# Attention into a two-expert mixture: x kept in token order, 16-byte routing records, later gathers, loads on two engines, a gate over four tiles

## The chip, the cores and the metric

The kernel runs on one core of one Trainium2 chip. The metric is the device time of that core in microseconds (us), the median of three runs. The engines are named as in the profile: PE is TensorE, DVE is VectorE, ACT is ScalarE, POOL is GpSimd and SP is SyncE; SPq and ACTq are the queues on which SP and ACT issue transfers.

## The reference

Two stages follow each other. The first is attention within chunks of 64 positions, for 8 batches and 8 heads of width 64. The second is a mixture of 8 experts over the 4608 tokens that the first one gives, in which each token goes to the two experts with the highest noisy logits.

```python
scores = q_c @ k_c.T / sqrt(64)                 # per batch, head and chunk of 64
attn = exp(scores - max); attn /= attn.sum() + 1e-9
x = (attn @ v_c)  as (4608, 512)                # one row a token, heads side by side
noisy = x @ w_gate + log1p(exp(x @ w_noise)) * noise          # (4608, 8)
top2 = the two largest; top2_w = softmax over these two
for e in range(8):
    out[mask] += top2_w * (relu(x[mask] @ w1[e]) @ w2[e])     # 512 -> 1024 -> 512
```

## The kernel before

**Attention.** The tokens are 36 tiles of 128. `attend(it)`, here called a turn, works on several tiles at once: scores of tile `it` (L355), probabilities times v of `it - 2` (`pv`, L381), the transposes of p of `it - 1` (`p_trans`, L371), the transposes of x of `it - 3` (`x_trans`, L396) and the gate logits of `it - 4` (`gate_mm`, L409), all of them on PE in this order. ACT copies the transposed p out of PSUM (`pts`, L373), takes the exponential (`pr`, L367) and copies the transposed x (`xt`, L400). VectorE takes the row maxima, subtracts them (L364), and normalises the product into a tile of x (`xs`). Each tile needs one load of q (`qb`, L320), two of k (`kb`, L322, a lower and an upper half of 64 rows) and two of v (`vb`, L327). SP issues all five, into rings of six buffers, three or four turns ahead.

**Routing.** The tiles form six groups of 4, 8, 4, 4, 8 and 8. When the logits of a group stand, a generator `route(g)` is started. `step_route` takes one VectorE instruction of it at a time at fixed places between other work. It ranks the tokens and gives each of a token's two choices a slot in the list of its expert. A GpSimd indirect transfer then scatters a tile's rows into DRAM (`slots`, L532), two transfers per token tile, 72 in all. A row is 2060 bytes: 512 values of x, a code (token number and second expert) and the two weights. Scatters have places of their own between other work (`scatter`), and a tiny copy or memset on GpSimd ahead of each (L528, L530) holds it back until the named buffer is written.

**Experts.** Each of 8 experts has three blocks of three or four tiles of 128 slots; the list of the blocks over all experts is numbered from 0. `layer1` forms relu(x W1) in eight column blocks of 128, `layer2` the product with W2, tile by tile. Values and weights are split into a high and a low part, and each product is three matmuls (`three`, L263). In layer 1, ACT writes the high part of the hidden values (`hh`, L276) and VectorE the residual (`hl`, L277); three PSUM banks are in turn. `weigh` (L283) multiplies a finished tile by its token weights and `store` adds it to the output through a GpSimd indirect transfer (L230). `w_load` (L107, L109) loads weights from SP and `w_split` splits them.

Blocks 0 and 1 belong to the first expert, and by `EARLY = {0: 2, 1: 4}` their slots are full as soon as the scatters of groups 2 and 4 have landed, block 2's with the last group's. Right behind these scatters SP loads the block's tiles (`xg`, L202) and the three columns of codes and weights (`meta0`). `resolve_early` turns these columns into row numbers and weights on VectorE, just ahead of the block's layer 2, where the store needs them. From block 3 on, SP loads each tile by an offset that is known only then (the expert's place), in four pieces of 32 rows (L207). VectorE transposes such a tile (L250), while PE transposes those of blocks 0 to 2 (L246). `resolve_all` gives the row numbers of all later blocks ahead of block 2's layer 2. Up to LEAD = 7 tiles are loaded ahead (`gather_more`).

**Order of the work.** The order is written out by hand: what the program names first is first on its engine. Turns 0 to 36 come first, then two `x_tile` (transpose and split of a tile of block 0), turn 37, the other `x_tile` and layer 1 of block 0. Inside that layer, `hook_tail` places the last two turns between the first matmuls, and `hook1` two scatters behind each column block. Layer 2 of blocks 0 and 1 has `hook2_r`: a scatter at every second step and the next block's `x_tile` at the places of `TURNS`. SP also writes 37 blocks of zeros into the output (`zero_out`) in that stretch.

## Time and profile before

| | value |
|---|---|
| time, median of 3 runs | 1029.89 us (1028.78 to 1033.22) |
| the profiled execution's own time | 1029.36 us |
| its span in the profile | 1027.6 us |
| PE, matmuls | 983.1 us busy, 96% |
| VectorE (DVE) | 446.1 us, 43% |
| ScalarE (ACT) | 271.3 us, 26% |
| GpSimd (POOL) | 227.4 us, 22% |
| mean granted clock of TensorE | 0.991 |
| DMA | mean 129 GB/s; HBM read 81.69 MB, written 50.13 MB |

A busy PE need not be PE at its peak, and a share of the whole span averages over two stages: attention with routing at the start, and the experts, which take most of the span. A row of the timeline has its start, its length (both in us), the engine, the line, the operation with output and inputs by their names, the tile's shape, and the count; in square brackets stands the idle time ahead of it and what ended it. A row of the table by stretches has the stretch and its length, then the busy time and the number of instructions of PE, of PE's weight loads, of VectorE, ACT and GpSimd, and then the granted clock, the DMA engines' mean share and the GB/s.

### The profile page before, as it was taken

The page shows a single profiled execution, that of the slowest core. Times are in us where ns is not written, and L with a number is a line of the kernel's source. Part 1 is how long each engine was busy: PE and PEld are TensorE (multiplying, and loading weights), DVE is VectorE, ACT ScalarE, POOL GpSimd, SP SyncE. Part 2 cuts the span into 40 slices and gives each one's busy share as a digit, 9 for nine tenths or more (in the row PEclk, how much of TensorE's full clock was granted, in tenths as well). Part 3 has the DMA queues.
Part 4 walks back from the last instruction along what each step waited for, and adds up shares of the span by engine and source line. Part 5 has one row for each costly group of instructions (what it writes and reads, how often), then busy time and mean ns, then how long its engine had stood idle before and what let it go on. Part 6 is the DMA issues. An engine that isn't in the chain of part 4 may idle for free.

```text
span 1027.6 us, 16132 instructions
## 1 busy us (share of the span) xinstructions
PE 983.1 (96%) x5962; PEld 883.5 (86%) x5962; DVE 446.1 (43%) x1005; ACT 271.3 (26%) x542; POOL 227.4 (22%) x332
## 2 busy tenths in 40 slices
PE   6889998999799999999999999999999999999996
PEld 6778887898689889888988998899889998999884
DVE  6656665522525443344334432453245324533311
ACT  3434443211314121222222321232123212322100
POOL 3034754751020111111111102101211111101112
PEclk9999999999899999999999999999999999999998
DMA  8899999864561552264225422553244324412213
GB/s 226 259 292 298 328 323 396 310 177 121 88 166 56 124 117 37 60 140 116 40 46 138 124 40 44 125 135 59 36 121 123 74 43 126 120 21 32 31 21 43
DMA packets 103218, 132.93 MB, mean 129 GB/s; under 512 B 22848, under 2 KB 56000, under 8 KB 103136
## 3 DMA queue, kind: packets, MB, share of 16 engines
q1 hardware_dynamic: 86704, 93.54, 30.4%
q0 software_dynamic: 16432, 38.33, 19.1%
q8 instruction: 48, 0.79, 0.3%
q14 instruction: 34, 0.28, 0.1%
HBM read 81.69 MB, written 50.13 MB: 128 GB/s over the span
## 4 chain that ended last, share of the span: by engine, by line
PE 84%; SPq 6%; DMA 5%; DVE 2%; issue 2%; ACT 1%; POOL 0%; DVEq 0%; ACTq 0%; POOLq 0%
PE PS L263 78%; DMA kb<-in_kT 2%; PE PS L381 2%; SPq L322 1%; PE PS L355 1%; SPq L327 1%; DMA xg<-slots 1%; DMA vb<-in_vh 1%; SPq L207 1%; PE PS L409 1%; PE PS L371 1%; SPq L320 1%; DMA out<-zero 1%; PE PS L396 1%; SPq L107 0%
## 5 line engine op out<-in xcount | busy, mean ns | idle before, releaser
L263 PE MATMUL PS<-xh,w1h 128*128 128x384 f32 (+2 forms) x768 | 262.6, 342 | 9.4 <-DVE hl L277 6.2
L230 POOL DMA_INDIRECT out<-o,lid x77 | 119.3, 1549 | 684.5 <-DVE o L283 680.3
L263 PE MATMUL PS<-xh,w1l 128*128 128x384 f32 (+2 forms) x768 | 261.7, 341 | 0.0
L263 PE MATMUL PS<-xl,w1h 128*128 128x384 f32 (+2 forms) x768 | 261.6, 341 | 0.0
L263 PE MATMUL PS<-w2h,hh 128*128 128x512 f32 x616 | 240.5, 390 | 0.0
L263 PE MATMUL PS<-w2h,hl 128*128 128x512 f32 x616 | 240.2, 390 | 0.0
L263 PE MATMUL PS<-w2l,hh 128*128 128x512 f32 x616 | 240.2, 390 | 0.0
L276 ACT ACTIVATE hh<-PS 128x384 fp32r<-128x384 f32 (+2 forms) x192 | 95.0, 496 | 481.0 <-PE PS L263 425.4
L277 DVE SCALAR_TENSOR_TENSOR hl<-PS,hh 128x384 fp32r<-128x384 f32 (+2 forms) x192 | 108.5, 566 | 188.4 <-ACT hh L276 185.5
L283 DVE TENSOR_SCALAR o<-PS,lwt 128x512 f32<-128x512 f32 x77 | 57.7, 749 | 248.6 <-PE PS L263 246.2
L263 PEld LDWEIGHTS PS<-xh,w1h 128*128 128x128 f32 x768 | 145.3, 189 | 12.7 <-DVE hl L277 6.6
L263 PEld LDWEIGHTS PS<-xl,w1h 128*128 128x128 f32 x768 | 145.4, 189 | 1.9
L263 PEld LDWEIGHTS PS<-xh,w1l 128*128 128x128 f32 x768 | 145.2, 189 | 1.1
L263 PEld LDWEIGHTS PS<-w2h,hl 128*128 128x128 f32 x616 | 112.9, 183 | 27.2
L263 PEld LDWEIGHTS PS<-w2l,hh 128*128 128x128 f32 x616 | 112.9, 183 | 26.2
L263 PEld LDWEIGHTS PS<-w2h,hh 128*128 128x128 f32 x616 | 112.9, 183 | 25.8
L532 POOL DMA_INDIRECT slots<-xs,lii x72 | 72.5, 1007 | 26.5 <-issue 20.8
L253 ACT ACTIVATE xh<-y 128x512 fp32r<-128x512 f32 x67 | 41.2, 614 | 105.5 <-DVE y L250 105.5
L254 DVE TENSOR_TENSOR xl<-y,xh 128x512 fp32r<-128x512 f32 x67 | 44.9, 670 | 47.9 <-ACT xh L253 47.2
L355 PE MATMUL PS<-kb,qb 128*64 128x128 f32 x576 | 40.9, 285 | 13.3 <-DMA kb<-in_kT 12.6
L250 DVE STREAM_TRANSPOSE y<-xg 128x512 f32<-128x512 f32 x67 | 45.6, 681 | 11.9 <-DMA xg<-slots 11.9
L381 PE MATMUL PS<-vb,pts 128*64 128x130 f32 x576 | 39.8, 278 | 9.3 <-ACT xt L400 5.6
(114 smaller groups left out, 686.7 us busy)
## 6 DMA issues: line engine op xcount, KB each, us to landing
st<-in_w SPq DMA_DIRECT2D x64, 512.0 KB
xg<-slots SPq DMA_DIRECT2D x252, 64.0 KB
out<-zero SPq DMA_DIRECT2D x37, 256.0 KB
vb<-in_vh SPq DMA_DIRECT2D x72, 130.0 KB
qb<-in_qT SPq DMA_DIRECT2D x36, 256.0 KB
kb<-in_kT SPq DMA_DIRECT2D x72, 128.0 KB
xg<-slots SPq DMA_DIRECT2D x9, 256.0 KB
slots<-zero SPq DMA_DIRECT2D x8, 257.5 KB
```

The lines of the kernel that those rows point to most:

```text
L207: nc.sync.dma_start(x[32 * q:32 * q + 32, 0:4 * r].rearrange("p (t c) -> p t c", c=P), by_slot[j * P:j * P + r, ds(place[e], 1), q * P:(q ...
L230: s = nc.gpsimd.indirect_dma_start(out=out, out_offset=bass.IndirectOffsetOnAxis(ap=rows_of(i, j)[0:r], axis=0), in_=o[0:r], in_offset=Non ...
L250: nc.vector.transpose(y[:, 0:4 * r], x[:, 0:4 * r])
L253: nc.scalar.activation(oh, src, AF.Copy)
L254: nc.vector.tensor_sub(ol, src, oh.bitcast(FT))
L263: nc.tensor.matmul(p, a, b, start=first and n == 0, stop=last and n == 2)
L276: nc.scalar.activation(hh[:, 0:n], p, AF.Relu)
L277: nc.vector.scalar_tensor_tensor(hl[:, 0:n], p, 0.0, hh[:, 0:n].bitcast(FT), op0=OP.max, op1=OP.subtract)
L283: nc.vector.tensor_scalar(o[0:r], p[0:r], weights_of(i, j)[0:r], None, op0=OP.mult)
L355: nc.tensor.matmul(PS[s, t % 2, hp * P:(hp + 1) * P], QB[t][:, hp, s], KB[t % RING][:, :, hp, s], start=True, stop=True)
L381: nc.tensor.matmul(PS[s, 3 + hp // 2, o:o + 130], PT[t][:, hp, s], VB[t % RING][:, :, c, hp, :], start=True, stop=True)
L532: s = nc.gpsimd.indirect_dma_start(out=slots, out_offset=bass.IndirectOffsetOnAxis(ap=lii[:, k, t0 + r:t0 + r + 1], axis=0), in_=XS[(t0 + ...
```

## The change

It has four parts.

1. **x stays in token order.** Finished tiles of x are stored to `xbuf` in DRAM, four at a time, from SP. A slot holds only the code and the two weights: 16 bytes, scattered from a small tile `mt` (L569 after the change) where the rows of 2060 bytes were scattered before. The number of scatters is the same. The buffers of x fall from 5 to 3 groups of four tiles.
2. **Tiles of x are gathered through the lists.** For blocks 0, 1 and 2, SP loads the list behind its last scatter; `finish_waiting` then resolves it on VectorE and has GpSimd gather the block's tiles from `xbuf` (`fetch_tile`, L216). It stands two turns behind the scatter, and, for what is still waiting, ahead of turn 36, in layer 2 of block 0 and in layer 1 of block 1. From block 3 on, GpSimd gathers a tile into a buffer `xr`, SP writes it to `sorted_x` in DRAM (`save`), and SP loads it from there in the four pieces as before, at a place known beforehand (`load_tile`). Up to FETCH = 6 tiles are gathered ahead. `resolve_all` moves from behind block 2's layer 1 into layer 2 of block 1. There, two scatters in three steps take the place of one in two.
3. **Loads on two engines.** The upper halves of k and v are issued by ACT.
4. **The gate over four tiles.** `x_copy` puts four tiles side by side. `gate_mm` then takes the gate's weights as the stationary operand and four tiles as the moving one, 512 columns, and each of the four slices of 128 input features writes 32 rows of a PSUM bank of its own. ACT copies that bank (`gate_copy`), and `gate_sum` adds the four slices per tile by a matmul with a matrix of ones and zeros (`sel`). A group's logits stand one turn later than before, and three turns are left for layer 1 of block 0.

The branch for lists that overflow, after the last block, is adapted in the same way.

```diff
+CODE, WA, WB = range(3)
...
+    xbuf = dram.tile([NROWS, DM], FT, name="xbuf")
+    slots = dram.tile([LROWS * NE, 4], FT, name="slots")
+    sorted_x = [[dram.tile([P, DM], FT, name=f"x{e}_{j}") for j in range(NLIST)] for e in range(NE)]
...
+    FETCH = 6
+    EARLY = {0: 2, 1: 4, 2: 5}
...
+    def save(keep=0):
+        while len(unsaved) > keep:
+            e, j, r, x = unsaved.pop(0)
+            nc.sync.dma_start(sorted_x[e][j][0:r], x[0:r])
+
+    def fetch_tile(i, k):
+        save(1)
...
+        nc.gpsimd.memset(spacer, 0.0)
         if i < NPE:
+            last = sum(groups[EARLY[i]])
+            x = XG[e, j] = xg.tile([P, DM], FT, name="xg")
+            nc.gpsimd.indirect_dma_start(
+                out=x[0:r], out_offset=None, in_=xbuf[0:P + last * P, :],
+                in_offset=bass.IndirectOffsetOnAxis(ap=rows_of(i, j)[0:r], axis=0))
+        else:
+            x = later_xg[1].tile([P, DM], FT, name="xr")
...
+            unsaved.append((e, j, r, x))
+
+    def load_tile(i, k):
...
         for q in range(4):
             nc.sync.dma_start(x[32 * q:32 * q + 32, 0:4 * r].rearrange("p (t c) -> p t c", c=P),
-                              by_slot[j * P:j * P + r, ds(place[e], 1), q * P:(q + 1) * P]
-                              .rearrange("(t p) o c -> p t (o c)", p=32))
+                              sorted_x[e][j][0:r, q * P:(q + 1) * P].rearrange("(t p) c -> p t c", p=32))
...
     def gather_more(most):
+        save()
         for _ in range(most):
+            if to_fetch and len(later) - len(to_fetch) < FETCH:
+                fetch_tile(*to_fetch.pop(0))
             if later and ahead[0] < LEAD:
-                gather_tile(*later.pop(0))
+                load_tile(*later.pop(0))
                 ahead[0] += 1
...
-        HT[i] = BH[0 if i == 1 else i % 2]
+        HT[i] = BH[i % 2]
...
-                nc.sync.dma_start(KB[t % RING][HALF[h], h], kT[HALF[h], t])
+                (nc.sync, nc.scalar)[h].dma_start(KB[t % RING][HALF[h], h], kT[HALF[h], t])
...
-                nc.sync.dma_start(VB[t % RING][HALF[h], h], vh[HALF[h], t])
+                (nc.sync, nc.scalar)[h].dma_start(VB[t % RING][HALF[h], h], vh[HALF[h], t])
...
     def x_copy(t):
+        g, r = divmod(t, 4)
+        if r == 0:
+            XT[g] = gx.tile([P, ND, 4, P], FT, name="xt", bufs=1)
+        nc.scalar.activation(XT[g][:, :, r, :], PS[:, 5, :].rearrange("p (d n) -> p d n", d=ND), AF.Copy)
...
-    def gate_mm(t):
-        for d in range(ND):
-            nc.tensor.matmul(lg_at(t), XT[t][:, d, :], wg[:, d, 0:16], start=(d == 0), stop=(d == ND - 1))
+    def gate_mm(g):
+        for d in range(ND):
+            nc.tensor.matmul(PS[32 * d:32 * d + 32, 6, :], wg[:, d, :], XT[g][:, d], start=True, stop=True)
+
+    def gate_copy(g):
+        LS[g] = gx.tile([P, 4, P], FT, name="ls")
+        nc.scalar.activation(LS[g].rearrange("p a b -> p (a b)"), PS[:, 6, :], AF.Copy)
...
+    def gate_sum(g):
+        for r in range(4):
+            nc.tensor.matmul(lg_at(4 * g + r), LS[g][:, r, :], sel, start=True, stop=True)
...
-                in_=XS[(t0 + r) // 4][:, r % 4, 0:USED], in_offset=None)
+                in_=mt[:, t0 + r, :], in_offset=None)
...
-                    gather(i)
                     early_loads.append(nc.sync.dma_start(
-                        meta0[i], by_slot[js * P:(js + m) * P, 0, CODE:USED].rearrange("(j p) c -> p j c", p=P)))
-            if g == LAST:
-                gather(len(EARLY))
+                        meta0[i], by_slot[js * P:(js + m) * P, 0, 0:3].rearrange("(j p) c -> p j c", p=P)))
+                    waiting.append((i, turn[0] + 2))
...
+    def finish_waiting():
+        while waiting:
+            i = waiting.pop(0)[0]
+            resolve_early(i)
+            gather(i)
...
+        if waiting and it >= waiting[0][1]:
+            finish_waiting()
...
+        gated = it - 4 >= 0 and (it - 4) % 4 == 3
+        if gated:
+            gate_mm((it - 4) // 4)
         if 0 <= it - 3 < NT:
             x_trans(it - 3)
-        if 0 <= it - 4 < NT:
-            gate_mm(it - 4)
-            if grp_of[it - 4] != grp_of.get(it - 3):
-                routing.append(route(grp_of[it - 4]))
+        if it - 5 >= 0 and (it - 5) % 4 == 3:
+            gate_sum((it - 5) // 4)
+            if grp_of[it - 5] != grp_of.get(it - 4):
+                routing.append(route(grp_of[it - 5]))
...
+        if gated:
+            gate_copy((it - 4) // 4)
...
+            if (it - 2) % 4 == 3:
+                u = (it - 2) // 4
+                nc.sync.dma_start(xbuf[P + 4 * u * P:P + (4 * u + 4) * P].rearrange("(a p) c -> p a c", p=P), XS[u])
...
     block_x(0)
     block_h(0)
+    finish_waiting()
     attend(NT)
...
-    tail = [NT + 2 + a for a in range(2)]
+    tail = [NT + 2 + a for a in range(3)]
...
+            if i == 1 and f == 2:
+                finish_waiting()
...
-            if f % 2 == 0:
+            if i == 0 and (k, f) == (0, 4):
+                finish_waiting()
+            if f % 3:
                 scatter(1)
+            if i == 1 and (k, f) == (0, 5):
+                resolve_all()
+                while len(to_fetch) > len(later) - FETCH:
+                    fetch_tile(*to_fetch.pop(0))
+                gather_more(1)
+            if i == 1 and k and f == 2:
+                gather_more(1)
...
-        if 1 < i < NBL and i == 3:
-            resolve_all()
+        if i == 3:
             layer2(i - 1, hook2_f)
...
-            resolve_early(0)
             layer2(0, hook2_r)
...
-            gather(3)
...
-            resolve_early(1)
             layer2(1, hook2_r)
```

Three places show what moves. First PE in attention. Before, a turn has five steps, the last being the gate of one tile (`wg` with `xt`, 128 rows by 16 columns).

```order
L355 MATMUL PS_101<-kb2_139,qb_327 64x128 x8
L381 MATMUL PS_101<-vb0_143,pts_504 64x130 x8
L371 MATMUL PS_101<-ident_65,pr_525 128x128 x4
L396 MATMUL PS_101<-ident_65,xs_471 128x128 x4
L409 MATMUL PS_101<-wg_202,xt_528 128x16 x4
L355 MATMUL PS_101<-kb3_140,qb_374 64x128 x8
```

After, about the same stretch of turns; `ls` is the copied bank of the gate and `sel` the matrix that adds it up.

```order
L384 MATMUL PS_186<-kb1_227,qb_375 64x128 x8
L410 MATMUL PS_186<-vb5_237,pts_531 64x130 x8
L400 MATMUL PS_186<-ident_146,pr_539 128x128 x4
L437 MATMUL PS_186<-xt_412,wg_291 32x512 x4
L425 MATMUL PS_186<-ident_146,xs_546 128x128 x4
L384 MATMUL PS_186<-kb2_228,qb_418 64x128 x8
L410 MATMUL PS_186<-vb0_232,pts_574 64x130 x8
L400 MATMUL PS_186<-ident_146,pr_586 128x128 x4
L425 MATMUL PS_186<-ident_146,xs_546 128x128 x4
L450 MATMUL PS_186<-sel_171,ls_589 128x16 x4
L384 MATMUL PS_186<-kb3_229,qb_460 64x128 x8
```

The gate's four matmuls are gone from each turn. Once in four turns there are four matmuls of 512 columns ahead of the transposes of x, and a turn later four with 16 columns behind them.

Next ACT in the same turns, before: three activations a turn, the copy of p, the exponential and the copy of x.

```order
L373 ACTIVATE pts_797<-PS_101 128x512
L367 ACTIVATE pr_809<-pr_809 128x512
L400 ACTIVATE xt_814<-PS_101 128x512
L373 ACTIVATE pts_848<-PS_101 128x512
L367 ACTIVATE pr_860<-pr_860 128x512
L400 ACTIVATE xt_865<-PS_101 128x512
```

After, with the names of the loads' buffers `kb` and `vb`:

```order
L349 DMA kb5_231<-in_kT 64x512
L354 DMA vb4_236<-in_vh 64x520
L402 ACTIVATE pts_574<-PS_186 128x512
L396 ACTIVATE pr_586<-pr_586 128x512
L441 ACTIVATE ls_589<-PS_186 128x512
L431 ACTIVATE xt_591<-PS_186 128x4x128
L349 DMA kb0_226<-in_kT 64x512
L354 DMA vb5_237<-in_vh 64x520
L402 ACTIVATE pts_623<-PS_186 128x512
```

Two loads stand ahead of each copy of p, and the copy of the gate's bank stands ahead of one copy of x in four.

Last GpSimd at the passage from layer 1 of block 0 to its layer 2. Before, the scatters of x rows (`xs`) run up to the first store of the block; `o` is a finished tile of the output.

```order
L532 DMA slots_62<-xs_1928,lii_80 44032x576
L528 MEMSET spacer_71 1x1
L532 DMA slots_62<-xs_1928,lii_80 44032x576
L528 MEMSET spacer_71 1x1
L532 DMA slots_62<-xs_1928,lii_80 44032x576
L528 MEMSET spacer_71 1x1
L532 DMA slots_62<-xs_1928,lii_80 44032x576
L229 MEMSET spacer_71 1x1
L230 DMA out_0<-o_2696,lid00_111 4736x512
```

After, `hh07` is the last hidden column block of layer 1, on which the last scatter with a copy ahead of it waits, and `lid01` is the resolved list of block 1:

```order
L567 COPY spacer_152<-hh07_2280 1x1
L569 DMA slots_63<-mt_297,lii_161 44032x4
L565 MEMSET spacer_152 1x1
L569 DMA slots_63<-mt_297,lii_161 44032x4
L565 MEMSET spacer_152 1x1
L569 DMA slots_63<-mt_297,lii_161 44032x4
L212 MEMSET spacer_152 1x1
L216 DMA xg_2714<-xbuf_62,lid01_197 128x512
L212 MEMSET spacer_152 1x1
L216 DMA xg_2717<-xbuf_62,lid01_197 128x512
L212 MEMSET spacer_152 1x1
L216 DMA xg_2720<-xbuf_62,lid01_197 128x512
```

Before, nothing but scatters stood ahead of the first store, since SP loaded the tiles of block 1. After, block 1's three gathers from `xbuf` stand in GpSimd's order behind two further scatters, and the other scatters and the stores stand behind them.

More of the change, by code (lines that the diff above doesn't have):

```diff
@@ L91 @@
     nc.vector.memset(caprow[:, 0:1], float(caps[0]))
+    sel = consts.tile([P, 16], FT, name="sel")
+    nc.vector.tensor_add(sel, ident[:, 0:16], ident[:, 32:48])
+    nc.vector.tensor_add(sel, sel, ident[:, 64:80])
+    nc.vector.tensor_add(sel, sel, ident[:, 96:112])
     run8 = consts.tile([P, NE], FT, name="run8")
@@ L211, in gather @@
     def gather(i):
         for k in range(len(blocks[BL[i][0]][BL[i][1]])):
-            gather_tile(i, k)
-    later = [(i, k) for i in range(4, NBL) for k in range(len(blocks[BL[i][0]][BL[i][1]]))]
-    ahead = [len(blocks[1][0])]
+            fetch_tile(i, k)
+    later = [(i, k) for i in range(NPE, NBL) for k in range(len(blocks[BL[i][0]][BL[i][1]]))]
+    to_fetch = list(later)
+    ahead = [0]
     def gather_more(most):
+        save()
         for _ in range(most):
+            if to_fetch and len(later) - len(to_fetch) < FETCH:
+                fetch_tile(*to_fetch.pop(0))
@@ L337 @@
     nc.sync.dma_start(nz, noise)
-    zero = consts.tile([P, USED], FT, name="zero")
+    zero = consts.tile([P, DM], FT, name="zero")
     nc.gpsimd.memset(zero, 0.0)
+    mt = consts.tile([P, NT, 4], FT, name="mt")
+    nc.gpsimd.memset(mt, 0.0)
     PR, PT, XS, XT, RC = {}, {}, {}, {}, {}
@@ L348, in x_at @@
         if r == 0:
-            XS[u] = rows.tile([P, 4, 520], FT, name="xs")
+            XS[u] = rows.tile([P, 4, DM], FT, name="xs")
         return XS[u][:, r]
@@ L426, in route @@
         ts = slice(t0, t0 + G)
-        parts = [(XS[t0 // 4 + a], slice(4 * a, 4 * a + 4)) for a in range(G // 4)]
         nc.scalar.activation(y, lg[:, :, 1, :], AF.Abs)
@@ L565 @@
     scatters = []
+    waiting = []
+    turn = [0]
+    def finish_waiting():
[3 more added lines that the diff above has]
+            gather(i)
     pending = []
@@ L597, in attend @@
             load_v(it + 3)
[L598 to L603 removed]
+        if it == 5:
+            nc.sync.dma_start(slots[0:NLIST * P * NE].rearrange("(p r) c -> p (r c)", p=P), zero[:, 0:NLIST * NE * 4])
+            nc.sync.dma_start(xbuf[0:P], zero)
+        turn[0] = it
+        if waiting and it >= waiting[0][1]:
+            finish_waiting()
         if it in (12, 14, 16, 18):
@@ L828 @@
             wo = ovp.tile([P, 1], FT, name="wo")
-            resolve(lo, wo, xm[:, None, CODE:USED],
+            resolve(lo, wo, mo[:, None, :],
                     lambda k: nc.vector.tensor_copy(k, pr[:, 0:1]),
                     lambda k, b: nc.vector.tensor_tensor(k, b, pr[:, 1:2], OP.is_equal))
-            xo = xm[:, 0:DM]
+            xo = ovp.tile([P, DM], FT, name="xo")
+            nc.gpsimd.indirect_dma_start(
+                out=xo, out_offset=None, in_=xbuf, in_offset=bass.IndirectOffsetOnAxis(ap=lo, axis=0))
             oo = ovp.tile([P, DM], FT, name="oo")
```

71 lines of the change are left out of this document (28 added, 43 removed).

## Prediction

> **What bounds the kernel now.** I read the page first, then busy time by stretch, then the timeline of TensorE (PE), whose gaps are what a change of loads and waits can win.
>
> ```profile
> span 1027.6 us, 16132 instructions
> PE 983.1 (96%) x5962; PEld 883.5 (86%) x5962; DVE 446.1 (43%) x1005; ACT 271.3 (26%) x542; POOL 227.4 (22%) x332
> ```
> ```profile
> 250.00:275.00 25.00, 18.82 (x81) 16.78 (x80) 8.03 (x14) 5.95 (x12) 0.00 (x0) 0.86 0.51 91
> 400.00:600.00 200.00, 200.00 (x994) 178.15 (x993) 79.90 (x131) 47.82 (x93) 31.61 (x40) 1.00 0.40 89
> ```
> PE is busy 983.1 of 1027.6, and from 400 to 600 wholly: the expert stage is at its floor, and the change leaves its matmuls alone. All idle time lies before 275: some in attention, one hole between 250 and 275. The timeline of PE, from the program's first scores to the first expert matmul, with one undisturbed turn in the middle:
>
> ```profile
> 5.52 3.43 PE L355 MATMUL PS<-kb,qb 128*64 128x128 f32 x32 [5.52 <-DMA kb<-in_kT]
> ...
> 24.85 1.09 PE L355 MATMUL PS<-kb,qb 128*64 128x128 f32 x16
> ...
> 34.77 1.11 PE L381 MATMUL PS<-vb,pts 128*64 128x130 f32 x16 [1.15 <-ACT xt L400]
> ...
> 41.93 1.09 PE L355 MATMUL PS<-kb,qb 128*64 128x128 f32 x16 [0.17 <-DMA kb<-in_kT]
> 42.85 1.06 PE L381 MATMUL PS<-vb,pts 128*64 128x130 f32 x16
> 43.84 0.66 PE L371 MATMUL PS<-ident,pr 128*128 128x128 f32 x4
> 44.33 0.60 PE L396 MATMUL PS<-ident,xs 128*128 128x128 f32 x4
> 44.77 0.96 PE L409 MATMUL PS<-wg,xt 128*128 128x16 f32 x8
> 45.66 1.09 PE L355 MATMUL PS<-kb,qb 128*64 128x128 f32 x16
> ```
> ```profile
> 154.00 1.09 PE L355 MATMUL PS<-kb,qb 128*64 128x128 f32 x16
> ```
> ```profile
> 167.31 0.44 PE L263 MATMUL PS<-xh,w1h 128*128 128x384 f32 x1 [1.41 <-DVE xl L254]
> ```
> A clean turn lasts 45.66 - 41.93 = 3.73, its gate 45.66 - 44.77 = 0.89. Turns 6 to 35 (24.85 to 154.00) are 29 in 129.15, 4.45 each: 21 us over the clean 108.2. Who held PE, in total:
>
> ```profile
> PE PS L355 <- DMA kb<-in_kT: 12.6, 10, 5.5
> ```
> Of these 12.6 the first 5.52 is the program's start, so 7.1 in nine waits is late k. Call the first expert matmul, 167.31, T0. The hole:
>
> ```profile
> 263.50 0.71 DVE L250 STREAM_TRANSPOSE y<-xg 128x512 f32<-128x512 f32 x1 [11.92 <-DMA xg<-slots]
> ```
> ```profile
> 266.19 0.74 PE L263 MATMUL PS<-xh,w1h 128*128 128x448 f32 x1 [6.18 <-DVE hl L277]
> ```
> ```profile
> 268.00:272.00 4.00, 4.00 (x14) 3.56 (x13) 3.30 (x6) 1.99 (x4) 0.00 (x0) 0.58 0.79 17
> 272.00:276.00 4.00, 4.00 (x21) 3.45 (x19) 1.93 (x8) 2.23 (x5) 0.00 (x0) 1.00 0.59 104
> ```
> VectorE stood 11.92 at block 3's first tile, its residual hl came late and PE stood 6.18. Then the clock was 0.58: 14 matmuls in 4 us where 21 fit. From 266.19 to 272 that is 5.8 x 0.4 = 2.3 more. The hole costs 8.5.
>
> **The change, part by part.** *Gate.* Four passes of 0.89 per four tiles go. In come gate_sum, four matmuls with 128-column weights like the old ones, 0.89, and gate_mm, four matmuls of 512 columns into 32 rows each. The nearest row is scores: eight of 128 columns into alternate 64 rows in 42.85 - 41.93 = 0.92, 0.115 each, 0.46 for 512 columns. The p transposes, 128 columns over all rows, take 44.33 - 43.84 = 0.49 for four records of one per matmul, 0.12 a record, and scores have two records per matmul: so 64-row halves overlap in pairs. Four in such pairs are 1.84, one half-pair over at the ends makes 2.1, which I take; alone 3.7, all four together 0.9. A turn becomes (4 x (3.73 - 0.89) + 2.1 + 0.89)/4 = 3.59, and 29 turns gain 4.1. The Trainium skill, "TensorE: Matmul & The Clock Gate", Part 3, says that matmuls in different column groups run at once, with a span of one matmul and about 4 ns per further tile; no row here shows more than two. By it gate_mm would be near 0.9 and nine passes 11 us cheaper than at 2.1.
>
> *Loads.* SP issues five loads per turn:
>
> ```profile
> 27.51 1.10 SPq L322 DMA_DIRECT2D kb<-in_kT  x2
> 28.71 1.18 SPq L327 DMA_DIRECT2D vb<-in_vh  x2
> ```
> ```profile
> 70.83 2.27 SPq L322 DMA_DIRECT2D kb<-in_kT  x2
> ```
> Two of them, some 1.1, go to ScalarE (ACT), ahead of p's copy. SP passes from about 2.9 to 1.7 per turn and the loads come earlier, so I book the 7.1 of late k as gone; what is late next is the route turn's wait (1.15 at 34.77), which stays. Queued behind the pair on ACT are three activations a turn:
>
> ```profile
> L367 ACT ACTIVATE pr<-pr 128x512 f32<-128x512 f32 x36 | 22.4, 623 | 10.1 <-DVE pr L364 10.0
> L373 ACT ACTIVATE pts<-PS 128x512 f32<-128x512 f32 x35 | 20.9, 597 | 77.3 <-PE PS L371 61.9 <-remote 6.7 <-PE PS L396 6.4
> L400 ACT ACTIVATE xt<-PS 128x512 f32<-128x512 f32 x33 | 19.3, 586 | 0.0
> ```
> 1.81 of work, and 77.3 of idle ahead of 35 copies, 2.2 each: the pair hides there. In turns with a weight split (0.62 more) or a route it may not: +1.2 in all (0 to 10). Turns 6 to 35: -4.1 - 7.1 + 1.2 = -10.0. Filling the pipeline: SP is quicker, but ACT issues nine loads (5 us) before its first exponential: -1.5 (+1 to -4). The turns after 35 lose two gates and gain a gate_sum: -0.9.
>
> *x rows and 16-byte writes.* The scatter count stays; each writes 16 instead of 2060 bytes. The DMA prices, for 110 to 130, 165 to 172 and 264 to 272:
>
> ```profile
> q0 software_dynamic: 663, 2.16, 29.5%
> ```
> ```profile
> q1 hardware_dynamic: 1247, 2.27, 84.8%
> ```
> ```profile
> q1 hardware_dynamic: 9286, 0.34, 71.1%
> ```
> Ten scatters (1280 rows) took 0.295 x 16 x 20 = 94 engine-us, 74 ns per long row; 12-byte reads 0.711 x 16 x 8/9286 = 9.8 ns. Plain transfers move 2.27/(0.848 x 7) = 0.38 MB/us. Loads (0.79 MB), the new x store (0.26) and weights (0.12) need 3.06 per turn; two scatters give an engine 16 rows: at 30 ns, which I take between the two, 3.5 in all, under the turn. Nothing booked; bounds 10 ns (nothing) and twice the long row (below). The x store holds SP for VectorE's normalisation once in four turns, with the next loads four turns ahead.
>
> *Early blocks, now gathered through lists.* Scatter, descriptor load, resolve on VectorE, GpSimd gather, then x_tile. Latencies and times:
>
> ```profile
> 224.11 0.97 POOL L532 DMA_INDIRECT slots<-xs,lii  x1 [0.22 <-issue]
> ```
> ```profile
> 226.94 1.94 SPq L202 DMA_DIRECT2D xg<-slots  x4
> ```
> ```profile
> 228.68 0.16 DVE L183 TENSOR_SCALAR rsa<-meta 128x3 int32<-128x3 int32 x1
> ...
> 229.94 0.16 DVE L191 TENSOR_TENSOR lwt<-lwt,rsw 128x3 f32<-128x3 f32 x1
> ```
> ```profile
> 193.75 1.43 POOL L532 DMA_INDIRECT slots<-xs,lii  x1 [0.15 <-issue]
> ```
> ```profile
> 199.24 0.60 PE L246 MATMUL PS<-ident,xg 128*128 128x128 f32 x4
> ```
> ```profile
> 210.20 0.33 PE L263 MATMUL PS<-xh,w1h 128*128 128x384 f32 x1
> ```
> A scatter lands 226.94 - 225.08 = 1.9 after GpSimd is done with it. I estimate 2.0 for a list load, 0.9 to the row numbers (1.4 for all of 228.68 to 230.10), 1.3 for a gather's issue (the 0.97 row and its memset), 2.2 to its landing: 9 with SP's issue. Block 0 has a turn and a half for its list: +1.0. Block 1 waits for scatter 56, now two scatters later in layer 1 of block 0, at the place of the row at 193.75: done at T0 + 27.9, tile landed at T0 + 36.9. PE wants it at 199.24 - 167.31 = T0 + 31.9, or + 33.1 with the gate's tail there (2.1 + 0.89 for two passes of 0.89: +1.2). A stall of about 4.0 (0 to 7). GpSimd, from T0 + 33.5 on, then has three gathers of 1.3, twelve scatters and two stores of 1.43 (24 us) up to the end of scatter 72, T0 + 57.5. Its list, which VectorE awaits behind hl of f = 2 in block 1, is resolved 5.5 later (the 9 less the gather's issue and landing), at T0 + 63. PE starts that block at T0 + 42.9 (the row at 210.20) + 1.2 + 4.0 = 48.1. The three PSUM banks let it do five column blocks of twelve matmuls at 0.2 (200 us for 994), to T0 + 60.2. That is 2.8, and an estimated 0.4 for hl itself: +3.2 (0 to 8). Slow clock after these: +2.3 (0 to 4).
>
> *Later blocks.* Lists, resolve and first gathers move up into layer 2 of block 1, to its sixth of eight steps: 48.1, eight column blocks of 2.4, 3.2, and 15 matmuls at 0.2 make T0 + 74. Resolve, gather, store, load and the queues of GpSimd and SP I estimate at 16 from the same latencies, so the first tile of block 3 lands near T0 + 90; PE ran dry at 266.19 - 6.18, T0 + 92.7. The hole goes: -8.5 (-8.5 to 0). Later tiles pass DRAM twice, six ahead of PE at some 11 us each; what hides 67 gathers is GpSimd's idle time (busy 31.61 of 200) and DMA at 0.40.
>
> Sum: -10.0 - 1.5 - 0.9 + 1.0 + 1.2 + 4.0 + 3.2 + 2.3 - 8.5 = -9.2. Against the profiled execution's 1029.36 (span 1027.6, 1.8 around it; the median is 0.5 above) that is 1020; its own range 1010 to 1030.
>
> **Rivals.** *A, small writes cost more than long rows, and it gets slower.* The DMA engines set the turn once 3.06 + 16p exceeds my turn of 3.59 + 0.5 of stalls that stay: p over 65 ns; all gain is lost at 88 ns. At twice the long row, 148 ns, a turn is 5.4, and 26 scattering turns lose 34: 1054. Against: 9.8 ns for small reads; for: no row isolates small writes to DRAM. The Trainium skill, "DMA: Bandwidth & Descriptors", Specifications, puts transfers under 512 B down as read-modify-write, which speaks for it.
>
> *B, ACT becomes attention's bound.* With copies of weights, route and gate ACT has about 2.3 a turn; a pair over 1.8 sets the pace. At the 2.27 of the row at 70.83, where SP waited for earlier loads, a turn is 4.6 and 29 lose 14: 1034. For: the pair waits for the same loads; against: most pairs take 1.10.
>
> *C, no new stalls, and gate_mm four at once.* 1020 - 9.5 - 11 = 1000. For: my latencies are estimates from busy queues.
>
> *D, later gathers come late* on GpSimd's queue: a hole of 8.5 per expert, up to 60 more. Against: the lead of six tiles.
>
> **How the numbers follow.** Forecast 0.55, A 0.12, B 0.13, C 0.15, D 0.05. Half a per cent, 5.1 us, is about what a measurement of this kernel can tell from no change. Three quarters of the forecast's range lie below 1024.2, a fifth within: faster 0.41 + 0.15 + 0.01 = 0.57; same 0.11 + 0.10 = 0.21; slower 0.03 + 0.12 + 0.05 + 0.02 = 0.22. The range 1000 to 1036 leaves out A, D and a little more.
>
> **What would show it.** Right: the first expert matmul near 157, no k wait after turn 6, gate_mm about 2.1, PE idle once before block 1's transposes and once in its layer 1, none near block 3. Wrong: k waits that stay with a full DMA (A); copies of p behind loads on ACT (B); gate_mm at 3.7; holes after 300 (D).

## The result and the profile after

The changed kernel takes 1061.91 us (median of 4, 1058.94 to 1063.58) beside 1029.93 before: 1.0302 times as long, interval 1.0266 to 1.0338. I had forecast 1020 and a range of 1000 to 1036. The profiled execution took 1063.58, its span is 1061.4, 33.8 more than before.

```profile
span 1061.4 us, 15625 instructions
PE 982.1 (93%) x5818; PEld 866.8 (82%) x5818; DVE 447.8 (42%) x1009; ACT 275.5 (26%) x551; POOL 313.1 (29%) x487
```
PE is busy for as long as before (982.1 us, 983.1 before), so the 33.8 lie in its idle time. The waits of PE by releaser (us in total, how often, the longest):

```profile
PE PS L291 <- DVE hl L305: 13.4, 2, 12.5
PE PS L410 <- ACT xt L431: 12.2, 6, 4.7
PE PS L410 <- ACT pts L402: 7.5, 3, 5.7
PE PS L274 <- DMA xg<-xbuf,lid: 6.8, 1, 6.8
PE PS L384 <- DMA kb<-in_kT: 5.8, 2, 5.3
```
Late k has gone but for the start, as forecast. In its place PE waits for ACT. Behind attention two holes stand where I had put one stall of 4 us and none. PE's timeline shows the places: the start, one gate, the last turns, and the experts.

```profile
20.20 2.00 PE L410 MATMUL PS<-vb,pts 128*64 128x130 f32 x16 [5.74 <-ACT pts L402]
...
33.24 1.09 PE L384 MATMUL PS<-kb,qb 128*64 128x128 f32 x16
...
38.79 1.07 PE L437 MATMUL PS<-xt,wg 128*32 128x512 f32 x8
39.79 0.66 PE L425 MATMUL PS<-ident,xs 128*128 128x128 f32 x4
```
```profile
160.79 2.00 PE L410 MATMUL PS<-vb,pts 128*64 128x130 f32 x16 [4.71 <-ACT xt L431]
```
```profile
164.64 1.22 PE L384 MATMUL PS<-kb,qb 128*64 128x128 f32 x16
```
```profile
178.18 0.44 PE L291 MATMUL PS<-xh,w1h 128*128 128x384 f32 x1 [1.46 <-DVE xl L282]
```
```profile
215.26 1.12 PE L274 MATMUL PS<-ident,xg 128*128 128x128 f32 x4 [6.79 <-DMA xg<-xbuf,lid]
```
```profile
296.74 0.74 PE L291 MATMUL PS<-xh,w1h 128*128 128x448 f32 x1 [12.52 <-DVE hl L305]
```
The gate's four matmuls of 512 columns take 39.79 - 38.79 = 1.0 together. Turn 6 starts at 33.24 (before 24.85), the last turn's scores at 164.64 (154.00), the first expert matmul, T0, at 178.18 (167.31). So 8.4 are lost in filling the pipeline, 2.3 in turns 6 to 35 (131.4 against 129.15), 0.2 up to T0, and 22.9 behind it (883.2 against 860.3).

The following table gives these pieces for every kernel that ran, from its profiled execution; ratios are to the kernel before on the same chip, whose median was 1026 to 1031 there. "T0" is the start of the first expert matmul; the last three columns are the time from turn 6 to the scores of turn 35, from there to T0, and from T0 to the end. The names are explained with the experiments. One of the four executions of fill_on_sp took 5505.44 us for a reason that stays open; it stands in the median, not in the ratio.

| kernel | median us | ratio, interval | turn 6 at | turns 6-35 | to T0 | behind T0 |
|---|---|---|---|---|---|---|
| before | 1029.93 | | 24.85 | 129.15 | 13.31 | 860.3 |
| changed | 1061.91 | 1.0302 (1.0266-1.0338) | 33.24 | 131.40 | 13.54 | 883.2 |
| gate4_before | 1020.40 | 0.9925 (0.9903-0.9948) | 25.07 | 120.16 | 12.06 | 858.7 |
| act_loads_before | 1036.24 | 1.0076 (1.0051-1.0102) | 35.57 | 129.22 | 11.98 | 859.9 |
| gate4_act_late | 1027.25 | 0.9976 (0.9956-0.9996) | 27.09 | 129.77 | 13.41 | 855.1 |
| x_store_before | 1045.62 | 1.0141 (1.0113-1.0168) | 23.90 | 139.05 | 12.12 | 868.8 |
| sp_loads | 1057.47 | 1.0281 (1.0257-1.0305) | 25.18 | 136.04 | 12.39 | 882.8 |
| fill_on_sp | 1062.18 | 1.0341 (1.0315-1.0368) | 27.97 | 137.32 | 12.34 | 881.6 |
| weights_first | 1061.58 | 1.0321 (1.0296-1.0345) | 34.35 | 129.12 | 12.10 | 885.6 |
| weights_late | 1044.32 | 1.0172 (1.0155-1.0189) | 34.59 | 131.08 | 12.00 | 867.2 |
| resolve_later | 1052.49 | 1.0260 (1.0236-1.0283) | 33.50 | 123.39 | 12.04 | 881.5 |
| late_both | 1048.26 | 1.0160 (1.0133-1.0187) | 33.70 | 126.41 | 20.60 | 866.0 |
| x_by_tile | 1045.59 | 1.0143 (1.0116-1.0170) | 33.48 | 126.77 | 17.35 | 865.3 |
| three_mended | 1040.77 | 1.0140 (1.0123-1.0157) | 27.05 | 130.75 | 13.07 | 868.7 |
| sp_two_mended | 1042.46 | 1.0114 (1.0087-1.0141) | 25.24 | 128.73 | 20.31 | 865.3 |
| x_store_twice | 1065.62 | 1.0325 (1.0298-1.0351) | 24.24 | 150.96 | 20.86 | 869.4 |
| scatter_twice | 1078.38 | 1.0467 (1.0437-1.0497) | 25.27 | 164.36 | 21.65 | 862.5 |

The pieces are rough, since each is from a single execution. The changed kernel, weights_first and weights_late run the same code up to T0 and reach it at 178.18, 175.57 and 177.67. Between resolve_later and late_both, which are also the same up to there, lie 11.8 us (168.93 and 180.71). A difference of two or three us between pieces says nothing, and a larger one needs a second run or the ratio beside it.

### The profile page after: what moved, and what is told of

It is laid out like the page before. It is cut to its first block, busy times and chain, and to the rows that moved or that the text cites. A ratio compares the mean times of both kernels' runs of the same rounds, so it can differ in the third digit from the quotient of the medians.

```text
span 1061.4 us, 15625 instructions
## 1 busy us (share of the span) xinstructions
PE 982.1 (93%) x5818; PEld 866.8 (82%) x5818; DVE 447.8 (42%) x1009; ACT 275.5 (26%) x551; POOL 313.1 (29%) x487
## 4 chain that ended last, share of the span: by engine, by line
PE 79%; DMA 10%; SPq 3%; another core or an unknown queue 2%; DVE 2%; issue 1%; ACT 1%; POOL 0%; ACTq 0%; POOLq 0%; DVEq 0%
PE PS L291 73%; SPq L634 3%; DMA kb<-in_kT 3%; DMA vb<-in_vh 2%; PE PS L410 2%; DMA x<-xr 1%; DMA qb<-in_qT 1%; PE PS L384 1%; PE PS L400 1%; DMA xbuf<-xs 1%; PE PS L425 1%; DMA slots<-mt,lii 1%; DMA meta<-slots 0%; DMA xr<-xbuf,lid 0%
## 5 line engine op out<-in xcount | busy, mean ns | idle before, releaser
L221 POOL DMA_INDIRECT xr<-xbuf,lid x67 | 67.5, 1008 | 135.5 <-DMA x<-xr 113.3
L569 POOL DMA_INDIRECT slots<-mt,lii x72 | 72.7, 1010 | 20.1 <-issue 18.9
L410 PEld LDWEIGHTS PS<-vb,pts 128*64 128x64 f32 x576 | 34.5, 143 | 36.9 <-ACT xt L431 13.4
```

What stands on the lines that cost most here:

```text
L221: nc.gpsimd.indirect_dma_start(out=x[0:r], out_offset=None, in_=xbuf, in_offset=bass.IndirectOffsetOnAxis(ap=rows_of(i, j)[0:r], axis=0))
L410: nc.tensor.matmul(PS[s, 3 + hp // 2, o:o + 130], PT[t][:, hp, s], VB[t % RING][:, :, c, hp, :], start=True, stop=True)
L569: s = nc.gpsimd.indirect_dma_start(out=slots, out_offset=bass.IndirectOffsetOnAxis(ap=lii[:, k, t0 + r:t0 + r + 1], axis=0), in_=mt[:, t0 ...
```

## The experiments

My theories, as the expectations name them: H, a load that ACT issues waits for earlier transfers to land, and ACT's copies stand behind it; W, the hole at block 3 comes from weight loads that hold a part of the engines; V, VectorE stands in the turn's order for block 0's list. The rivals: F, the DMA engines are full in attention whoever issues; A of the prediction, small writes are dear. X, that the store of x takes the time which the loads lack, came after the first eight runs.

**The gate and the loads, each alone.** The first kernel is the one before with `x_copy`, `gate_mm`, `gate_copy`, `gate_sum` and their places as in the change, and nothing else of it (gate4_before).

> The kernel before with only the gate over four tiles. Its PE work is some 0.4 us a turn less (3.6 for four old passes against 1.9 for the new ones). If PE and its chain set the turn: 11 to 13 us off, 1017 to 1020. Theory F (DMA engines full): the turns stay at 4.4, the waits for k grow from 5.6 us in turns 6 to 35 to 15 or more, 1027 to 1031.

It is faster than both kernels: 0.9925 (0.9903 to 0.9948). The turns fall by 9.0, to 120.16, and the waits for k hardly move (5.6 us in the turns before, 5.0 now, quoted below). The two rows for the turns, before first (the last three figures are the granted clock, the DMA engines' share and GB/s):

```profile
24.85:154.00 129.15, 114.69 (x1427) 105.22 (x1426) 82.66 (x321) 56.77 (x126) 55.02 (x86) 0.99 0.97 300
```
```profile
25.07:145.23 120.16, 105.45 (x1306) 87.25 (x1305) 85.63 (x318) 61.05 (x133) 52.60 (x82) 0.97 0.99 315
```
PE's busy time falls by 9.2 and the turns with it. Theory F's forecast, turns that stay at 4.4 and long waits for k, did not come. Its premise did: the engines' mean share is 0.97 before and 0.99 with the gate alone. Even so they moved 315 GB/s where it had been 300.

The next one has the loads alone:

```diff
-                nc.sync.dma_start(KB[t % RING][HALF[h], h], kT[HALF[h], t])
+                (nc.sync, nc.scalar)[h].dma_start(KB[t % RING][HALF[h], h], kT[HALF[h], t])
...
-                nc.sync.dma_start(VB[t % RING][HALF[h], h], vh[HALF[h], t])
+                (nc.sync, nc.scalar)[h].dma_start(VB[t % RING][HALF[h], h], vh[HALF[h], t])
```

> The kernel before with only the upper halves of k and v moved to ACT. Theory H: slower by 8 us in filling and by 5 to 10 in the turns, where ACT's copies wait: 1043 to 1048. Theory F: filling alone, 1036 to 1040, turns as before (4.45). If what I booked in the prediction holds (late k goes, ACT hides the pair): 1022 to 1024.

The filling lost 10.7 and the turns nothing: 1.0076. That is what theory F had forecast, and not what I had booked (1022 to 1024). Why the filling suffers shows in the changed kernel's timeline of ACT: its first exponential stands behind nine loads, and the copy of p behind two more that wait.

```profile
0.77 1.19 ACTq L349 DMA_DIRECT2D kb<-in_kT  x2
...
10.23 0.47 ACTq L354 DMA_DIRECT2D vb<-in_vh  x1
10.75 0.63 ACT L396 ACTIVATE pr<-pr 128x512 f32<-128x512 f32 x1 [8.73 <-DMA vb<-in_vh]
18.21 0.47 ACTq L349 DMA_DIRECT2D kb<-in_kT  x1
19.03 0.47 ACTq L354 DMA_DIRECT2D vb<-in_vh  x1
19.55 0.60 ACT L402 ACTIVATE pts<-PS 128x512 f32<-128x512 f32 x1 [8.16 <-DMA wg<-in_wgn]
```
An issue costs 0.47 or a little more. Seven issues take 3.65 of the 8.73 and two take 0.94 of the 8.16; most of the rest is waiting for earlier transfers to land, SP's load of `wg` among them. The records of the trace show why: the loads of SP and of ACT share eight counters of landings, and each issue waits for the transfer that used its counter last, about eight places before it, whichever engine issued that one. The chain of the changed kernel shows ACT held by SP's store of x in this way:

```profile
104.73 8.42 DMA xbuf<-xs
113.17 0.47 ACTq L349
```
Then the two together, with the first five tiles' loads left on SP:

```diff
+                (nc.sync, nc.scalar if t > 4 else nc.sync)[h].dma_start(KB[t % RING][HALF[h], h], kT[HALF[h], t])
...
+                (nc.sync, nc.scalar if t > 4 else nc.sync)[h].dma_start(VB[t % RING][HALF[h], h], vh[HALF[h], t])
```

> The kernel before with the gate over four tiles and with the upper halves of k and v on ACT from the sixth tile on. If ACT's loads cost only where they fill the pipeline, and late k (5.0 us in the turns) goes: 1015 to 1019 beside 1020 for the gate alone. If ACT's copies of p then stand behind loads as long as k did: 1020 to 1024.

The turns are back at 129.77, where the gate alone has 120.16: 9.6 us, the whole gain of the gate. By the ratios the loads cost half of that (0.9976 against 0.9925), and the time is above both forecasts. There ACT's copies stand behind loads, and no wait for k is left among PE's waits in the turns; PE waits for `xt` (7.9), `pts` (4.9) and `pr` (2.2) instead. In act_loads_before the turns did not grow; that the longer turn covered the same delay there is argued, not shown.

**The changed kernel with loads on SP.** The reverse of the diff above, applied to the changed kernel.

> The changed kernel with all five loads of a turn issued by SP again. Theory H (a load that ACT issues waits for an earlier transfer to land, and the copies of p stand behind it): the 8.4 us lost in filling the pipeline come back, and the waits of PE for ACT in the turns (some 24 us, against 8 before) fall to about 10, so the first expert matmul comes near 160 instead of 178, and the time is 1043 to 1048. Theory F (the DMA engines are full in attention, whoever issues): only the filling comes back, the turns stay at 4.4 to 4.5 us each, the waits move to k on SP; first expert matmul near 169, time 1052 to 1054. Rival A (16-byte writes are dear): nothing comes back in the turns and the GpSimd queue's share of the DMA engines is over 5% there; time over 1055.

Neither theory: the filling is mended (25.18), the turns are longer by 4.6 (136.04), with 13.8 us of waits for k and a stop of 9.93 for `xt` before the last turn. 1.0281 against 1.0302. Rival A's time came (over 1055), but not its sign: the share of the GpSimd queue is 1.2%, not over 5%. With only the first five tiles on SP:

> The changed kernel with the loads of the first five tiles issued by SP and only the later upper halves by ACT. Theory H, in the form that is left (ACT's loads cost the filling alone, since there its first exponentials stand behind loads that wait for others to land): turn 6 starts near 25 instead of 33.2, the turns after it stay at 4.5 each, and the time falls by 7 to 9 from the changed kernel's 1061.9: 1053 to 1055. Rival (ACT's loads cost in every turn as well, or the wait at the start is that of a full DMA whoever issues): turn 6 stays after 30, 1058 or more.

Turn 6 starts 5.3 earlier and turns 6 to 35 last 5.9 longer: nothing is left at T0 (177.63 against 178.18). The rival's time came (1058 or more), though not its sign (turn 6 after 30): what the filling gives back is lost again in the turns.

**The store of x.** The kernel of gate4_before, with x stored to a spare buffer as in the change, beside its long rows:

```diff
             norm_c(it - 2)
+            if (it - 2) % 4 == 3:
+                u = (it - 2) // 4
+                nc.sync.dma_start(xbuf[P + 4 * u * P:P + (4 * u + 4) * P].rearrange("(a p) c -> p a c", p=P), XS[u][:, :, 0:DM])
```

> The kernel before with the gate over four tiles, and with x stored in token order beside its long rows, which stay in use (the copy is not read). Theory X: the turns grow from 120 by 8 to 25 and the time from 1020 to 1028 to 1045, with late k as the wait that grows. If the store of x is hidden: 1019 to 1023.

The turns grow by 18.9, from 120.16 to 139.05 (and block 1's tiles come later: 868.8 behind T0). The wait for k in turns 6 to 35, first of the gate alone, then with the store:

```profile
PE PS L359 <- DMA kb<-in_kT: 5.0, 4, 2.1
```
```profile
PE PS L360 <- DMA kb<-in_kT: 15.8, 9, 4.8
```
That is 10.8 of the 18.9. The rest is PE at a lower clock (granted 0.90, with the gate alone 0.97), busy for 7.8 more with the same matmuls:

```profile
23.90:162.95 139.05, 113.25 (x1306) 94.20 (x1306) 85.70 (x319) 61.18 (x134) 54.00 (x84) 0.90 0.99 329
```
The changed kernel drops the long rows, so it was repeated there. The base has all loads on SP and the two edits of the next part (sp_two_mended); on it the store is made twice, the second time to a spare buffer.

> The changed kernel with all loads on SP, the weights late and block 0's resolve one turn later; the base for the next two. Turns 6 to 35 took 136.0 with all loads on SP, 11 to 12 of it at the resolve: now some 125, the first expert matmul near 162, 865 to 867 behind it: 1029 to 1033. If two queues are what makes the turns of the changed kernel long, the turns fall to 120 as in the kernel before with the gate alone, and the time to 1024 to 1027.

> The kernel of sp_two_mended with each group of four tiles of x stored a second time, to a spare buffer. Theory X (the store of x, 1 MB in one piece four tiles at a time, takes DMA time that the loads of the turns lack): the turns grow by 10 us or more (9.4 MB at some 0.3 MB per us are 31 us of all engines, of which the slack hides a part), time up by 8 to 30. If the store is hidden: under 3 us more. Rival A (the 16-byte writes are what slows the transfers): under 3 us more.

The base missed its forecast (1029 to 1033): T0, which I had put near 162, came at 174.28. Its turns take 128.73, which is 139.05 - 128.73 = 10.3 less than x_store_before. That is not the price of the long rows alone, since behind the turns the base has a stop of 4.4 with a slower clock, where block 0's list and gathers now stand, and the piece to T0 takes 20.31 instead of 12.12:

```profile
163.11 2.00 PE L410 MATMUL PS<-vb,pts 128*64 128x130 f32 x16 [4.41 <-ACT ls L441]
```
At T0 only 0.8 of the 10.3 is left (174.28 against 175.07). The second store costs 22.2 more in the turns, with waits for k of 26.7 instead of 7.7, and T0 moves by 21.8:

```profile
PE PS L384 <- DMA kb<-in_kT: 7.7, 4, 3.0
```
```profile
PE PS L385 <- DMA kb<-in_kT: 26.7, 8, 6.0
```
Is it the volume, or the megabyte in one piece? On late_both (below), x was stored tile by tile instead:

```diff
-            if (it - 2) % 4 == 3:
-                u = (it - 2) // 4
-                nc.sync.dma_start(xbuf[P + 4 * u * P:P + (4 * u + 4) * P].rearrange("(a p) c -> p a c", p=P), XS[u])
+            u = it - 2
+            nc.sync.dma_start(xbuf[P + u * P:P + (u + 1) * P], x_at(u) if u % 4 else XS[u // 4][:, 0])
```

> The kernel of late_both with x stored tile by tile, 256 KB in every turn, instead of 1 MB once in four turns. If the cost of the store is its volume: within 4 us of late_both. If it is the manner (a megabyte in a row ahead of the loads, so that loads come late in bursts): the turns fall by 6 us or more and the time with them.

The turns take 126.77 against 126.41: the volume. What loads, weights and store move together, from the DMA queue of sp_two_mended between 100 and 125 (packets, MB, share of 16 engines), is 6.91/(0.958 x 25) = 0.289 MB/us:

```profile
q1 hardware_dynamic: 3876, 6.91, 95.8%
```

**The 16-byte writes (rival A).** In the same stretch the changed kernel's scatters show

```profile
q0 software_dynamic: 288, 0.02, 1.2%
```
A packet is not a write. Nine scatters are issued there, which is 9 x 128 = 1152 rows of 16 bytes, or 0.018 MB; the trace's packets hold eight rows each. So a write costs 0.012 x 16 x 25 x 1000/1152 = 4.2 ns of an engine, where a long row took 74, counted in the same way. (The 16 to 17 ns of the expectations are the time of one packet.) To look for a cost that packets don't show, each scatter of attention was made twice on the base, the second into a spare list:

```diff
+            if turn[0] < NT:
+                s2 = nc.gpsimd.indirect_dma_start(
+                    out=slots2, out_offset=bass.IndirectOffsetOnAxis(ap=lii[:, k, t0 + r:t0 + r + 1], axis=0),
+                    in_=mt[:, t0 + r, :], in_offset=None)
...
```

> The kernel of sp_two_mended with each scatter of attention done a second time, into a spare list. Rival A (a 16-byte write costs the engines or the memory much more than the 16 to 17 ns that its packets show): the turns grow by 5 us or more. By the packets' time alone: some 50 scatters of 128 rows at 17 ns on 16 engines are 7 us of one-sixteenth shares, under 1 per cent of the engines: the turns stay within 2 us and the time within 3, but for what GpSimd itself, 1.3 us more per scatter, holds up.

The turns grew to 164.36, as rival A wants it, yet not by the DMA: in the stretch from 125 to 145 its share is 0.68, and GpSimd is busy for 17.01 of 20 us.

```profile
125.00:145.00 20.00, 15.94 (x160) 12.75 (x160) 11.00 (x45) 7.42 (x15) 17.01 (x23) 0.85 0.68 184
```
So the run says that four scatters a turn are too much for GpSimd, and nothing of small writes; it was badly chosen. Against A stand the 4.2 ns, and a base that with its short rows is no later at T0 than the kernel with long ones.

**The wait for block 0's list.** VectorE's order holds the resolve ahead of the next row maxima, and the list waits for its last scatter to land. The chain of the changed kernel:

```profile
147.32 5.92 DMA slots<-mt,lii
153.26 2.42 DMA meta<-slots
157.05 0.69 DVE mx L388
```
```diff
-                    waiting.append((i, turn[0] + 2))
+                    waiting.append((i, turn[0] + 3))
```

> The changed kernel with block 0's resolve one turn later. Theory V (VectorE stands in the turn's order for a list that waits for the last scatter to land, and holds the row maxima of the turn): PE's stop of 4.7 us before the last turn falls under 1.5 and the slow clock behind it goes; the first expert matmul comes 4 to 7 us earlier: 1055 to 1058. Rival (the list is only as late as DMA lets it be, and the tiles of block 0 then come late): the stop moves to the transposes of block 0, 1060 to 1064.

T0 is 9.3 earlier, 1.0260. The stop of 4.71 is gone, and the slow stretch behind it. The scatter landed 5.9 after its issue instead of the 1.9 that I had taken; the DMA engines' share is 1.05 from 147.3 to 153.2. With all loads on SP VectorE waits longest for this list, and the same edit takes that wait away (sp_two_mended):

```profile
151.99 0.17 DVE L188 TENSOR_SCALAR rsa<-meta 128x3 int32<-128x3 int32 x1 [8.18 <-DMA meta<-slots]
```
The gain in time is not sure. By the ratios it is 0.4%, and with the weights late as well (late_both, below) T0 comes 3.0 later, not earlier.

**The weight loads (theory W).** They were first moved ahead of the list loads:

```diff
+            for c in range(4):
+                w_load(1, 1, c)
             for r in range(NE):
                 nc.sync.dma_start(meta[:, :, r], by_slot[0:NJ * P, ds(place[r], 1) if r else slice(0, 1), 0:3]
                                   .rearrange("(j p) o c -> p j (o c)", p=P))
-            for c in range(4):
-                w_load(1, 1, c)
```

> The changed kernel with the next expert's weight loads issued ahead of the eight list loads instead of behind them. Theory W (the first three saves of gathered tiles take 15.6 us to land since parts of them stand behind the weight loads, which trickle on a quarter of the engines until they are done): the weights are through some 12 us earlier, the saves land in 2 to 4 us, and PE's stop of 12.5 us at block 3 falls to 0 to 5: 1051 to 1056. Rival (the lists and GpSimd's gathers are late by themselves): the stop stays at 10 or more, or the lists land later by what the weights take of the queue: 1060 or more.

No gain: PE's stop moved to block 2's tiles, 21.4 us, whose gathers and the list loads now were the ones behind the weights. The issues of the eight list loads, of the changed kernel and of this one:

```profile
240.94 8.75 SPq L802 DMA_DIRECT2D meta<-slots  x8
```
```profile
244.47 23.83 SPq L804 DMA_DIRECT2D meta<-slots  x8
```
So the theory's remedy was wrong, as its rival had said: the lists landed later by what the weights took. Then the weights went behind the first tiles, into layer 1 of block 2:

```diff
+            if i == 2 and f == 0:
+                for c in range(4):
+                    w_load(1, 1, c)
...
-            for c in range(4):
-                w_load(1, 1, c)
```

> The changed kernel with the next expert's four weight loads behind the saves and first loads of gathered tiles, in layer 1 of block 2. Theory W (every transfer that is spread over the engines lands only when the weight loads on four of them are through): the saves land in 2 to 4 us, the hole of 12.5 us at block 3 falls to 4 or less and no hole of over 10 us appears elsewhere, the slow clock behind it goes too: 1047 to 1053. Rival (the gathers are late by their place in GpSimd's order or the lists): the hole stays at 8 or more, 1058 or more.

1.0172, and 867.2 behind T0 instead of 883.2. The issues of the saves and of the first loads, changed kernel first:

```profile
262.97 24.90 SPq L206 DMA_DIRECT2D x<-xr  x6
287.96 4.14 SPq L232 DMA_DIRECT2D xg<-x  x8
```
```profile
255.93 12.01 SPq L206 DMA_DIRECT2D x<-xr  x6
268.03 3.89 SPq L232 DMA_DIRECT2D xg<-x  x8
```
In the changed kernel a save took 15.55 us to land, while between 270 and 280 the queue shows a quarter of the engines busy:

```profile
264.98 15.55 DMA x<-xr
```
```profile
q1 hardware_dynamic: 304, 1.03, 25.5%
```
Four weight loads of 512 KB at 26 KB/us on each of four engines take 20 us. No view shows the engines one by one, but the trace records every part's landing. The four weight loads land in four parts each, one load behind the other: complete at 261.1, 269.3, 274.3 and 279.4. The save issued at 262.97 lands in sixteen parts: twelve by 266.5, the other four from 279.2 to 279.9. The two saves behind it do the same. In weights_late all sixteen parts of the first save land within 3.9 us of its issue. So the weight loads queue up on four engines, and a save that is spread over sixteen is done only when its parts on these four have come through. Theory W's cause is shown. Whether the four come from the load's source, whose rows the code splits in four (`j=4`), was not tried.

**Together.** Weights late and resolve later, with the loads as changed:

> The changed kernel with the weights late and block 0's resolve one turn later, ACT keeping its loads; the base for the next. If the two costs are separate: 1061.9 less 17 and 9, so 1033 to 1038. If they cover each other: 1041 or more.

1.0160, hardly better than the weights alone (1.0172). The gain of the later resolve didn't add up: the piece from turn 35 to T0 grew from 12 to 20.6, with a stop of 4.3 for `ls`. With the first loads on SP as well:

> The three edits together: the first loads on SP, the weights late, the resolve one turn later. If the three costs are separate: 1062 less 8, 11 and 5, so 1036 to 1042, still slower than before by the stop at block 1 (6.8) with its slow clock, the shorter one in its layer 1, and late k in the turns. If one of them covers another: 1046 or more.

1.0140. It reaches T0 at 170.87, resolve_later with all loads as changed at 168.93: the filling is 6.5 shorter and the turns are 7.4 longer. All versions that store x stay above 1.01; the gate alone stays the fastest.

## Why the prediction was wrong, point by point

The forecast was 9.2 down, and it went 33.8 up. Of the 43.0 between, 22.3 lie ahead of T0 (booked -11.4, measured +10.9) and 20.7 behind it (booked +2.2, measured +22.9). Two steps failed above all, one on each side: "Nothing booked" for the store of x, and "The hole goes" for the later blocks.

- *Gate.* Right in kind, too small in size. I took 2.1 for the four wide matmuls and a gain of 4.1 in the turns; they take 1.0, and the turns fall by 9.0 in gate4_before. The rule that I had weighed against it (the Trainium skill, "TensorE: Matmul & The Clock Gate", Part 3, matmuls in different column groups run at once) is what this trace shows.
- *x rows and 16-byte writes: "Nothing booked".* This is the step that failed ahead of T0. I let loads, store and weights share 0.38 MB/us, a rate taken from the writes of zeros; with loads in the mix the queue moves 0.289. Even the answer from which I took the long rows, 110 to 130 of the kernel before, has 4.32/(0.714 x 20) = 0.303:

```profile
q1 hardware_dynamic: 2530, 4.32, 71.4%
```
At 0.289 the 0.79 + 0.26 + 0.12 MB need 4.05 a turn instead of 3.06, and 16 writes of 4.2 ns add 0.07: 4.1, above my turn of 3.59. Turns of sp_two_mended measured 128.73/29 = 4.44. In the runs the store took 18.9 (x_store_before) and 22.2 (x_store_twice) in the turns, where I had nothing. Still, this sum is not the whole mechanism. For the gate alone, between 100 and 125, it gives 0.91/(5.47/(0.699 x 25)) + 16 x 0.086 = 4.3, the 0.086 being 0.330 x 16 x 25/1536 for the rows of twelve scatters. The turn there is 4.14. So the sum doesn't hold the step from 4.14 to 4.44, and that stays open:

```profile
q1 hardware_dynamic: 3211, 5.47, 69.9%
```
```profile
q0 software_dynamic: 955, 3.15, 33.0%
```
- *Loads.* Late k went, as booked, though only 5.6 of the 7.1 lay in turns 6 to 35. But I priced the pair on ACT by its issue (1.1) and by one row of 2.27, and its wait is the landing of other transfers. In the filling that is +8.4 where I had -1.5 (bounds +1 to -4). In the turns rival B's mechanism is there: 9.6 in gate4_act_late, where the rival had 14. Beside the store of x it is not what sets the turns: with all loads on SP they are 4.6 longer.
- *Block 0's list: +1.0.* In the changed kernel a stop of 4.7 and a slow stretch; 8.0 in the turns by resolve_later, and nothing at T0 by late_both. Its price alone isn't shown.
- *Block 1: a stall of 4.0.* The latencies held: the transposes start at T0 + 37.1, I had T0 + 36.9. PE came there earlier, so the stop is 6.8. It stays in every version with the lists.
- *Block 2's resolve: +3.2.* PE lost 3.5 there, between 234 and 239, but not for the list: ACT's first `hh` of that layer started at 237.86, 7.7 after the end of its matmuls (see below).
- *Later blocks: the hole goes, -8.5.* This is the step that failed behind T0. I counted 16 us from resolve to landing as if nothing else were on the DMA engines then. A save alone took 15.6, behind the weight loads. The hole grew to 12.5, and 16.0 of the 22.9 behind T0 come back with weights_late.
- *Rival A* had the right sign, 1054, for the wrong reason. The rule that had spoken for it (the Trainium skill, "DMA: Bandwidth & Descriptors", Specifications, on transfers under 512 B) gives no dear writes here: 4.2 ns a write beside 74 a long row. Per byte the small writes are the slower, 3.8 bytes a ns of an engine against 28, which agrees with the page; that they are read-modify-writes no run shows.

The kernels before, gate4_before, x_store_before, sp_two_mended, sp_loads and changed form a chain. Along it turns 6 to 35 go -9.0, +18.9, -10.3, +7.3 and -4.6, in all +2.3. The sum closes because each step is the difference of two neighbours, so it proves nothing by itself. T0, which counts filling and last turns too, goes -10.0, +17.8, -0.8, -0.7 and +4.6, in all +10.9. So the -10.3 and the +7.3 are for the most part a stop that lies within the turns in one kernel and behind them in the other. What holds in both readings is the gain of the gate and the price of the store. With the 22.9 behind T0 the 10.9 make the 33.8.

Shown are the costs of the store, of ACT's loads in the filling and with the gate alone, and of the weights' place. Not shown are the price of the short rows alone and that of block 0's list alone. Not tried was a mending of block 1's stop; its list waits for scatter 56, the fourteenth of the 16 that GpSimd issues in that layer, and these would have to start earlier.

## What to carry to other kernels

A transfer's price is what it takes from the other transfers in its stage; take the rate from a stretch with the same mix, not from one with writes alone. An engine that computes pays for a load not only the issue but the landing of whatever the load must wait for. Before an early transfer is put on a path, look at what long transfer is on the engines at that moment, and put the long one behind it.

## What the runs showed of the hardware

In several places an engine started long after the one that it waited for had finished, and the profile names no releaser. In the changed kernel `hh` waited until 237.86 for matmuls that the timeline ends by 230.2, and PE itself ran single matmuls with gaps and no wait:

```profile
234.85 0.33 PE L291 MATMUL PS<-xh,w1l 128*128 128x384 f32 x1 [0.84 <-issue]
235.59 0.42 PE L291 MATMUL PS<-xh,w1h 128*128 128x384 f32 x1 [0.41 <-issue]
237.00 0.33 PE L291 MATMUL PS<-xl,w1h 128*128 128x384 f32 x1 [0.98 <-issue]
```
```profile
237.86 1.26 ACT L304 ACTIVATE hh<-PS 128x384 fp32r<-128x384 f32 x3 [11.03 <-remote]
```
Until 236.5 GpSimd had issued gathers, scatters and stores without a pause. The same gaps fill the turns of scatter_twice, where GpSimd never rests, and an unnamed wait of 5.7 ahead of `pts` lies in the 20.6 of late_both. Against GpSimd as the cause stands resolve_later: from 155.3 to 165.5 it issues three gathers and five scatters without a longer pause, and no such stop comes. Whether GpSimd holds the others up was not separated; it stays open.
